# An unused tile that moves the high side of SBUF by 1376 bytes, in a kernel of attention and two MLPs

## The chip, the cores and the metric

The kernel runs on one core of a Trainium2 chip. The core has five engines with queues of their own: TensorE (PE in the rows, with its weight loads as PEld), VectorE (DVE), ScalarE (ACT), GpSimd (POOL) and SyncE (SP), which issues nearly all DMAs here. The engines work on tiles in SBUF, whose 128 partitions each have their own run of bytes, so a tile has one byte address that is the same in all its partitions. TensorE reads a moving and a stationary operand from SBUF and accumulates in PSUM. The metric is the device time of one execution in microseconds (us).

## What is computed

Attention with a feature map (batch 4, 8 heads, 576 rows of 64), then two MLPs on the 2304 rows of 512 that come out of it. In short:

```
phi(x): proj = x @ w_phi; proj -= max|proj| of the row; concat(exp(proj), exp(-proj))
attn:   kv = phi(k)^T v, z = sum of phi(k);  x = (phi(q) kv) / (phi(q) z + 1e-6)
mlp 1:  h = (x @ w1) * (x @ w2);  y = (h @ w3) @ w_out        (512 -> 1024 -> 1024 -> 512)
mlp 2:  r = max(y @ w_in, 0);     out = (r * r) @ w_out2      (512 -> 2048 -> 512)
```

The weights of the MLPs come as 64-bit floats and are taken apart on the chip.

## The kernel before

All of it is one function, `attention_then_mlps`, and the order of instructions on every engine is written out by hand. To keep fp32 accuracy with the faster fp32r matmul, each operand is a tile `[128, 2, 512]` of a high part and a low part, 2048 bytes each. A product is three passes: high by high, low by high, high by low (`passes`). With four blocks of 128 along the contraction, or four blocks of output, that makes **runs of 12 matmuls**, each with a weight load of its own: 128 columns of stationary operand (512 bytes of a partition), then 512 moving columns (256 for the block of the tails).

The work has three stages.

- **Attention**, until about 200 us, with decoding of the first weights beside it.
- **MLP 1**: 40 steps, of which 32 have 512 moving columns and 8 have 256. A step has a run `pa` (L179, in `wide`), a run `pb` (L179) and, one step behind, a run `yp` (L883, in `fold_in`). In the first eight steps there is also `pf` (L840, two runs of 12 in a row), which folds w3 into w_out, and before `yp` the transposes `pw` (L173) for it.
- **MLP 2**: 80 steps, of which 64 have 512 columns and 16 are of the tails. A step has a run `ph` (L179) and, one step behind, `op` (L901, in `last_product`; in the 16 steps of the tails it is only 6 matmuls).

Between the runs, ScalarE and VectorE make the next moving or stationary operand from PSUM: in MLP 2 `t` (L1035), `r` (L1037, L1043 for the high part, L1045 for the low part).

**Where tiles lie.** Pools are opened on one of two sides: the low side is filled from the bottom of SBUF upward, the high side (`side="right"`) from the top downward, and each keeps its buffers from then on. On the low side are the identity matrix, the raw weights and decoding temporaries (`stage`), 20 buffers of 4096 bytes (`units`, made by `unit`) and the 5 operand buffers of `place` (`mid`). On the high side lies first `att` (all that attention needs beyond these) and, when that is closed, `late`: 12 buffers of 4096 bytes, the `t`, `g32` and `g` buffers, and two sets of decoding temporaries.

```python
att = actx.enter_context(tc.tile_pool(name="att", bufs=2, side="right"))
late = ctx.enter_context(tc.tile_pool(name="late", bufs=2, side="right", reuse_waits="tile"))
```

The sides of the operands of each run, by the addresses in the built program (moving, then stationary):

| run | moving operand | stationary operand |
|---|---|---|
| `pa`, `pb` L179 | block of x, low side | w1 or w2, low side |
| `ph` L179 | block of y, low side | w_in, low side |
| `pf` L840 | w_out, low side | w3 turned, low side |
| `yp` L883 | `g`, high side | `w3o` (folded weights), high side |
| `op` L901 | w_out2: 12 of 16 high side, 4 of 16 low side | `r`, high side |

A high part on the low side starts at 2688 modulo 4096, on the high side at 4064 (buffers of 2048 bytes, and all low parts, at 640 and 2016). Both sides have one offset for all their operand tiles of the MLPs.

Of the kernel before, what the change touches and what calls it, by code (L numbers as in the profile page):

```python
# [9 lines left out]
F32 = mybir.dt.float32  # L10
# [7 lines left out]
P = 128  # L18
C = 4
TAIL = 64  # L20
LEFT = 20
RIGHT = 12

# [18 lines left out]
def attention_then_mlps(ctx: ExitStack, tc: tile.TileContext, q, k, v, w_phi, w1, w2, w3, wo, wi2, wo2, out):  # L44
# [15 lines left out]
    units = ctx.enter_context(tc.tile_pool(name="units", bufs=1))  # L60
    mid = ctx.enter_context(tc.tile_pool(name="mid", bufs=1))
    dram = ctx.enter_context(tc.tile_pool(name="dram", bufs=1, space=bass.MemoryType.DRAM))

    def unit(dtype, shape, name):
        return units.tile([P] + shape, dtype, tag="u", bufs=LEFT, name=name)
# [134 lines left out]
    with ExitStack() as actx:  # L200
# [488 lines left out]
        with tc.manual_schedule(engines=mine):  # L689
            for entry in START:  # L690
                name, t = entry.split("/")
# [15 lines left out]

    def lunit(dtype, shape, name, tag="w", bufs=RIGHT):
        return late.tile([P] + shape, dtype, tag=tag, bufs=bufs, name=name)
# [4 lines left out]

    free = {"u": LEFT - 18, "w": RIGHT}
    home, given = {}, []
# [376 lines left out]
```

## Time and profile before

| | |
|---|---|
| device time, median of three runs | 951.58 us (950.89, 951.58, 952.81) |
| the profiled execution: span from first to last instruction | 952.7 us |
| TensorE busy | 931.8 us, 98% |
| VectorE, ScalarE, GpSimd busy | 545.8, 382.4, 249.5 us |
| granted TensorE clock, mean | 0.998 |

Of the profiled execution the page gives the span alone; it lies inside the range of the three runs and 1.1 us above their median. In the rows, a busy TensorE is not yet TensorE at its peak: matmuls overlap, and the length of a row reaches to the modelled end of its last matmul. What a run really takes is the distance from its start to the start of the next run.

### The profile page before, as it was taken

Reading aid. Unit: us, or ns where it says so; the run is one execution under the profiler, and the core shown is the slowest. Engines: PE = TensorE matmul, PEld = TensorE weight load, DVE = VectorE, ACT = ScalarE, POOL = GpSimd, SP = SyncE. Lnnn points to the kernel's source line nnn. Section 1 sums busy time; section 2 is a strip of 40 time slices with the busy share of each in tenths; the row PEclk is TensorE's granted clock in tenths of the full one; section 3 lists DMA queues with packets and bytes.
Section 4 is the critical chain, followed back from the end, with each engine's and each line's share of the span. In section 5 each row is a group of like instructions: output and inputs, shape, how many; then the busy total and the mean of one; then the engine's idle time right before and its main releaser. Section 6 shows DMA issues by size and latency. Waiting matters only on the chain.

```text
span 952.7 us, 14857 instructions
## 1 busy us (share of the span) xinstructions
PE 931.8 (98%) x5915; PEld 764.0 (80%) x5915; DVE 545.8 (57%) x892; ACT 382.4 (40%) x689; POOL 249.5 (26%) x304
## 2 busy tenths in 40 slices
PE   8899998999999999999999999999999999999997
PEld 7677776778888988888988888888888888888896
DVE  5898889778656456666856678852224223322332
ACT  4777777643322333432333344342223223222322
POOL 1565566454121123333423245520000000000000
PEclk9999999999999999999999999999999999999999
DMA  6565566144241334254452333211002000100000
GB/s 166 125 159 151 136 158 199 55 153 157 87 133 55 124 110 155 67 199 155 164 187 91 132 126 96 89 41 48 1 1 89 1 0 1 67 1 1 29 17 22
DMA packets 81109, 89.22 MB, mean 94 GB/s; under 512 B 44624, under 2 KB 65680, under 8 KB 81040
## 3 DMA queue, kind: packets, MB, share of 16 engines
q1 hardware_dynamic: 79712, 87.72, 29.7%
q8 instruction: 46, 0.75, 0.3%
q10 hardware_dynamic: 1328, 0.56, 0.3%
q14 instruction: 23, 0.19, 0.1%
HBM read 69.76 MB, written 18.35 MB: 92 GB/s over the span
## 4 chain that ended last, share of the span: by engine, by line
PE 89%; DVE 4%; ACT 3%; DMA 2%; issue 1%; SPq 0%; ACTq 0%
PE op L901 21%; PE ph L179 21%; PE yp L883 11%; PE pb L179 10%; PE pa L179 10%; PE pf L840 5%; PE po L455 2%; PE pk L246 2%; PE pq L376 2%; PE pkv L428 2%; DMA mrow<-mh 2%; ACT qp L417 2%; PE pd L477 1%; DVE kmax L344 1%; DVE m L383 1%; ACT kp L361 1%
## 5 line engine op out<-in xcount | busy, mean ns | idle before, releaser
L901 PE MATMUL op<-w_w,r 128*128 128x512 f32 x864 | 213.8, 395 | 0.1
L901 PEld LDWEIGHTS op<-w_w,r 128*128 128x128 f32 x864 | 161.3, 188 | 36.8 <-ACT r L1043 0.5
L179 PE MATMUL ph<-y,w_w 128*128 128x512 f32 (+1 forms) x768 | 165.5, 365 | 0.0
L1037 DVE SCALAR_TENSOR_TENSOR r<-ph,t 128x512 f32<-128x512 f32 (+1 forms) x80 | 51.0, 638 | 194.0 <-ACT t L1035 194.0
L179 PEld LDWEIGHTS ph<-y,w_w 128*128 128x128 f32 x768 | 133.3, 188 | 25.8
L1035 ACT ACTIVATE t<-ph 128x512 f32<-128x512 f32 (+1 forms) x80 | 44.5, 556 | 222.2 <-PE ph L179 222.2
L883 PE MATMUL yp<-g,w3o 128*128 128x512 f32 (+1 forms) x480 | 107.6, 373 | 0.0
L883 PEld LDWEIGHTS yp<-g,w3o 128*128 128x128 f32 x480 | 83.8, 188 | 16.0
L125 POOL TENSOR_TENSOR dt_w<-dt_w,dy_w 128x512 f32<-128x512 f32 x48 | 62.9, 1310 | 126.8 <-DVE dy_w L120 126.7
L179 PE MATMUL pa<-c,w_w12a 128*128 128x512 f32 (+1 forms) x432 | 94.4, 368 | 0.0
L179 PE MATMUL pb<-c,w_w12b 128*128 128x512 f32 (+1 forms) x432 | 93.6, 366 | 0.0
L179 PEld LDWEIGHTS pa<-c,w_w12a 128*128 128x128 f32 x432 | 75.1, 188 | 14.2
L179 PEld LDWEIGHTS pb<-c,w_w12b 128*128 128x128 f32 x432 | 75.2, 189 | 13.0
L1045 DVE TENSOR_TENSOR r<-r,r 128x512 fp32r<-128x512 f32 (+1 forms) x80 | 51.0, 638 | 41.3 <-ACT r L1043 35.6
L962 DVE TENSOR_TENSOR g<-pb,a 128x512 f32<-128x512 f32 (+1 forms) x39 | 24.8, 636 | 85.9 <-PE pb L179 81.3
L135 POOL TENSOR_TENSOR w_w<-dt_w,w_w 128x512 fp32r<-128x512 f32 x32 | 48.9, 1528 | 86.8 <-ACT w_w L133 86.8
L1043 ACT ACTIVATE r<-r 128x512 fp32r<-128x512 f32 (+1 forms) x80 | 47.2, 590 | 55.5 <-DVE r L1037 55.5
L502 POOL TENSOR_SCALAR rc<-dc 32x9 f32<-32x9 f32 x128 | 45.4, 355 | 58.8 <-DVE dc L492 51.8
L964 ACT ACTIVATE g<-g 128x512 fp32r<-128x512 f32 (+1 forms) x39 | 23.0, 589 | 91.6 <-DVE g L962 91.6
L954 ACT COPY a<-pa 128x512 f32<-128x512 f32 (+1 forms) x39 | 21.2, 543 | 83.1 <-PE pa L179 83.1
L361 ACT ACTIVATE kp<-kp 128x512 f32<-128x512 f32 (+1 forms) x80 | 46.9, 588 | 17.2 <-DVE kp L354 14.8
L117 DVE TENSOR_SCALAR dy_w<-dt_w 128x512 int32<-128x512 int32 x48 | 51.1, 1064 | 0.7
(135 smaller groups left out, 1285.3 us busy)
## 6 DMA issues: line engine op xcount, KB each, us to landing
x<-x_hbm SPq DMA_DIRECT2D x16, 512.0 KB
raw_w<-in_moe_w_dram SPq DMA_DIRECT2D x16, 512.0 KB
raw_w<-in_moe_w_in_dram SPq DMA_DIRECT2D x16, 512.0 KB
raw_w<-in_moe_w_out_dram SPq DMA_DIRECT2D x16, 512.0 KB
qm<-in_q_dram SPq DMA_DIRECT2D x32, 128.0 KB
km<-in_k_dram SPq DMA_DIRECT2D x16, 256.0 KB
vs<-in_v_dram SPq DMA_DIRECT2D x32, 128.0 KB
raw_wo<-in_moe_w_out_dram SPq DMA_DIRECT2D x8, 512.0 KB
```

Of the source, the lines that this page charges most:

```text
L117: nc.vector.tensor_scalar(out=e, in0=t, scalar1=-(1 << 23), scalar2=None, op0=ALU.bitwise_and)
L125: nc.gpsimd.tensor_tensor(out=w, in0=t.bitcast(F32), in1=e.bitcast(F32), op=ALU.add)
L135: nc.gpsimd.tensor_tensor(out=dst[:, 1], in0=w[0], in1=dst[:, 0].bitcast(F32), op=ALU.subtract)
L179: nc.tensor.matmul(ps[:, 0:n], a, c, start=kk + i == 0, stop=kk == KD - 1 and i == 2)
L361: nc.scalar.activation(z["kp", j][:, :, s, :], z["kp", j][:, :, 1, :], AF.Exp, scale=1.0 - 2.0 * s)
L502: nc.gpsimd.tensor_scalar(out=z["rc2"][i * 32:(i + 1) * 32, s, :], in0=z["dc"][at * 32:(at + 1) * 32, :], scalar1=1e-6, scalar2=None, op0= ...
L840: nc.tensor.matmul(pf, a, c, start=g + j + n == 0, stop=g == 1 and j == 3 and n == 2)
L883: nc.tensor.matmul(blk.yp[i][:, 0:blk.n], a, d, start=c % HG + s == 0, stop=c % HG == HG - 1 and s == 2)
L901: nc.tensor.matmul(ops[i], a, d, start=j + s == 0, stop=j == NR - 1 and s == 2)
L1037: nc.vector.scalar_tensor_tensor(out=r32[:, 0:n], in0=ph[:, 0:n], scalar=0.0, in1=t[:, 0:n], op0=ALU.max, op1=ALU.mult)
L1043: nc.scalar.activation(r[:, 0, 0:n], r32[:, 0:n], AF.Copy)
L1045: nc.vector.tensor_tensor(out=r[:, 1, 0:n], in0=r32[:, 0:n], in1=r[:, 0, 0:n].bitcast(F32), op=ALU.subtract)
```

## The change

A pool `skew` is opened on the high side ahead of all others there, with one tile of 344 floats (1376 bytes of each partition) that nothing writes or reads. As that side is filled downward, every other tile of it lies 1376 bytes lower. The low side, PSUM and the buffers in DRAM stay where they were.

```diff
+SKEW = 344
...
     units = ctx.enter_context(tc.tile_pool(name="units", bufs=1))
     mid = ctx.enter_context(tc.tile_pool(name="mid", bufs=1))
     dram = ctx.enter_context(tc.tile_pool(name="dram", bufs=1, space=bass.MemoryType.DRAM))
+
+    skew = ctx.enter_context(tc.tile_pool(name="skew", bufs=1, side="right"))
+    skew.tile([P, SKEW], F32, name="skew")
```

No instruction is added, removed or moved: on all five engines the order is the same, waits included, with source lines 4 later (L179 is then L183, L883 L887, L901 L905, L840 L844) and other numbers in the names. What differs is the addresses, as the built programs have them:

| tiles | before | after |
|---|---|---|
| low side, operand tiles (high part, low part), modulo 4096 | 2688, 640 | 2688, 640 |
| high side in the MLPs: weights, `g`, `r`, `w3o` (high part, low part), modulo 4096 | 4064, 2016 | 2688, 640 |
| high side in the MLPs: `t`, `a`, `g32`, modulo 4096 | 4064 or 2016 | 2688 or 640 |
| distance of high side to low side, modulo 2048 | 1376 | 0 |
| the same, modulo 64 | 32 | 0 |

In attention the tiles of the high side have many sizes, so they have no single offset before or after; each lies 1376 bytes lower.

## Rows read from the trace of the kernel before

**Rows 1.** The page: busy time, the span in 40 slices, the chain that ended last.

```profile
PE 931.8 (98%) x5915; PEld 764.0 (80%) x5915; DVE 545.8 (57%) x892; ACT 382.4 (40%) x689; POOL 249.5 (26%) x304
...
PEclk9999999999999999999999999999999999999999
...
PE 89%; DVE 4%; ACT 3%; DMA 2%; issue 1%; SPq 0%; ACTq 0%
```

**Rows 2.** Timeline of PE, MLP 1, all operands low: start, length, line, matmuls.

```profile
265.00 2.88 PE L840 MATMUL pf<-w_wo,w3T 128*128 128x512 f32 x12
267.71 2.88 PE L179 MATMUL pa<-c,w_w12a 128*128 128x512 f32 x12
270.44 2.88 PE L179 MATMUL pb<-c,w_w12b 128*128 128x512 f32 x12
273.16 0.38 PE L173 MATMUL pw<-ident,dt_w 128*128 128x128 f32 x2
```

**Rows 3.** Timeline of PE, two steps of MLP 1 without `pf`.

```profile
356.22 2.88 PE L179 MATMUL pb<-c,w_w12b 128*128 128x512 f32 x12
358.94 2.94 PE L883 MATMUL yp<-g,w3o 128*128 128x512 f32 x12
361.72 2.92 PE L179 MATMUL pa<-c,w_w12a 128*128 128x512 f32 x12
364.48 2.89 PE L179 MATMUL pb<-c,w_w12b 128*128 128x512 f32 x12
367.20 1.09 PE L883 MATMUL yp<-g,w3o 128*128 128x512 f32 x4
```

**Rows 4.** Timeline of PE, MLP 2: w_out2 high at 751.98, low at 757.52 and 763.06.

```profile
749.21 2.93 PE L179 MATMUL ph<-y,w_w 128*128 128x512 f32 x12
751.98 2.94 PE L901 MATMUL op<-w_w,r 128*128 128x512 f32 x12
754.75 2.93 PE L179 MATMUL ph<-y,w_w 128*128 128x512 f32 x12
757.52 2.97 PE L901 MATMUL op<-w_w,r 128*128 128x512 f32 x12
760.32 2.90 PE L179 MATMUL ph<-y,w_w 128*128 128x512 f32 x12
763.06 2.97 PE L901 MATMUL op<-w_w,r 128*128 128x512 f32 x12
765.86 0.40 PE L179 MATMUL ph<-y,w_w 128*128 128x512 f32 x1
```

**Rows 5.** Timeline of PE: the first and the last `ph` around MLP 2's 64 steps.

```profile
544.23 1.55 PE L179 MATMUL ph<-c,w_w 128*128 128x512 f32 x6
...
898.79 1.59 PE L179 MATMUL ph<-y,w_w 128*128 128x256 f32 x12
```

**Rows 6.** Timeline of PE, a step of MLP 1 with `pf` (`pa`, `pb`: rows 2).

```profile
262.23 5.64 PE L840 MATMUL pf<-w_wo,w3T 128*128 128x512 f32 x24
...
273.95 3.02 PE L883 MATMUL yp<-g,w3o 128*128 128x512 f32 x12
276.81 5.42 PE L840 MATMUL pf<-w_wo,w3T 128*128 128x512 f32 x23
```

**Rows 7.** Timeline of PE, 256 columns: a step of MLP 1, then the tails of MLP 2.

```profile
321.41 1.60 PE L179 MATMUL pa<-c,w_w12a 128*128 128x256 f32 x12
322.85 1.60 PE L179 MATMUL pb<-c,w_w12b 128*128 128x256 f32 x12
324.29 1.60 PE L883 MATMUL yp<-g,w3o 128*128 128x256 f32 x12
325.73 1.60 PE L179 MATMUL pa<-c,w_w12a 128*128 128x256 f32 x12
...
915.73 1.56 PE L901 MATMUL op<-w_w,r 128*128 128x512 f32 x6
917.12 1.59 PE L179 MATMUL ph<-y,w_w 128*128 128x256 f32 x12
918.55 1.56 PE L901 MATMUL op<-w_w,r 128*128 128x512 f32 x6
```

**Rows 8.** Timeline of DVE, then of ACT, in one step of MLP 2.

```profile
748.72 0.69 DVE L1045 TENSOR_TENSOR r<-r,r 128x512 fp32r<-128x512 f32 x1 [0.70 <-ACT r L1043]
752.87 0.69 DVE L1037 SCALAR_TENSOR_TENSOR r<-ph,t 128x512 f32<-128x512 f32 x1 [3.46 <-ACT t L1035]
...
752.24 0.60 ACT L1035 ACTIVATE t<-ph 128x512 f32<-128x512 f32 x1 [3.55 <-PE ph L179]
```

**Rows 9.** Busy time of PE until 189 us: matmuls, granted clock, DMA share, GB/s.

```profile
0.00:189.00 189.00, 173.77 (x2276) 0.99 0.55 144
```

**Rows 10.** Waits of PE, the two longest: us in total, times, longest.

```profile
PE pq L410 <- DMA mrow<-mh: 7.5, 6, 2.7
PE pq L376 <- ACT qp L417: 3.9, 5, 0.9
```

**Rows 11.** Groups by form, 256 moving columns: attention, then MLP 2 (busy, mean ns).

```profile
L246 PE MATMUL pk<-wbd,kT 128*128 128x256 f32 x192 | 27.0, 290 | 0.0
...
L179 PE MATMUL ph<-y,w_w 128*128 128x256 f32 x192 | 25.4, 282 | 0.0
```

## What was predicted before the run

> **What bounds the kernel now.** I read the page first. TensorE is busy 98% of the span at full granted clock, and the chain that ended last is 89% TensorE [rows 1]. After attention nothing else stands on that chain for long, so from about 200 us on the time is the number of matmuls times what one takes. The question is then what one takes, and whether it hangs on where its operands lie. For that I went to the timeline of TensorE and read it from start to start of the runs, since the length of a row contains the pipeline's end.
>
> There are two paces for the same shape (128x128 weights, 512 columns). **Settled:** from 265.00 to 273.16 stand 36 matmuls in a row (half of `pf`, then `pa`, `pb`), all operands on the low side. They take 8.16 us, 226.7 ns each, though `pf`, `pa` and `pb` have three different weights, two different moving blocks and three PSUM banks [rows 2]. **Disturbed:** a plain step of MLP 1 is also 36 matmuls, `yp` and then `pa` and `pb`, from 358.94 to 367.20: 8.26 us. In it `yp` (high side) takes 2.78, `pa` (low, right behind it) 2.76, and `pb` (low, behind a low run) 2.72 [rows 3]. A run that follows one from the other side is slow; a run that follows one from its own side is not.
>
> MLP 2 alternates low `ph` and high `op` without a second run to settle in. A step takes 5.54 us: 2.77 and 2.77 where both operands of `op` are high (749.21 to 754.75), and 2.80 and 2.74 where its moving operand is low and its stationary one high (757.52 to 763.06) [rows 4]. 24 settled matmuls would be 8.16 x 24/36 = 5.44. Nothing differs between these two kinds of step but the address of w_out2. That moves 0.03 us from one run to the other, which I take as the best sign that addresses of the two operands act on each other.
>
> The Trainium skill speaks against this. In "SBUF — State Buffer", section "Who interferes with whom", TensorE has two independent read ports, one for the moving operand and one for the weights, and never waits for anyone. By that the place of w_out2 could not show, and here it does, by 2.80 against 2.77 [rows 4].
>
> **The change part by part.** It adds no instruction and no wait, and keeps the order of all engines. It moves all tiles of the high side by 1376 bytes, so that operands of both sides have the same offset modulo 2048 (and 64). Every run of the MLPs then stands, modulo 4096, just as the low runs stand to each other in rows 2. I do not know which modulus counts; low runs settle whichever low buffers they use and whichever 512-byte slice of weights comes next, so the modulus that counts divides 512, and by any such modulus the two sides are 352, 96 or 32 bytes apart before and 0 after.
>
> My theory: a pair of operands with different offsets disturbs the overlap of weight load and stream, and after a change of side it takes most of a run to settle again. With one offset there is no change of side. The sum, in differences against the profiled execution's span of 952.7:
>
> - Plain steps of MLP 1 with 512 columns: 8.26 - 8.16 = 0.10 us [rows 2, 3]. There are 32 steps with 512 columns; 8 have `pf`, so 24 x 0.10 = 2.4.
> - Steps with `pf`: the first 24 matmuls of `pf` take 267.71 - 262.23 = 5.48, settled 5.44; `yp` takes 2.86 behind the transposes, settled 2.72 [rows 2, 6]. 0.04 is due to the change of side; of the 0.14 of `yp` I give half to the change of side (0.06 is what a plain `yp` has over 2.72 [rows 3]) and the rest to the transposes ahead of it. 0.10 a step, seven of them (the first lies among attention's last products): 0.7. I count 0.4, since the share of the transposes is a guess.
> - MLP 2 with 512 columns: from 544.23 to 898.79 are 64 steps in 354.56 us [rows 5], 5.54 each, so 64 x (5.54 - 5.44) = 6.4.
> - 256 columns: a step of MLP 1 takes 325.73 - 321.41 = 4.32, 1.44 for each run, the low behind low `pb` too: nothing to gain. A step of the tails in MLP 2 takes 918.55 - 915.73 = 2.82 against 1.44 + 6 x 0.2267 = 2.80 [rows 2, 7]: 16 x 0.02 = 0.3.
> - Attention: there the operands have many offsets before and after. One product has a like in the MLPs: `pk`, moving high, stationary low, 256 columns, has a mean of 290 ns against 282 for `ph` with 256, waits included [rows 11]. 192 x 8 ns = 1.5 us is the most that I give it, on either side of zero, because the settled pace of 256 columns was no better than the disturbed one [rows 7]. TensorE idles 15 us until 189 us [rows 9], partly for DMAs (7.5) and ScalarE (3.9) [rows 10], and a little saved there is lost in those waits. I take 0.
> - VectorE, ScalarE, GpSimd, DMAs: the low part of `r` ends at 749.41 and `op` starts to use it at 751.98 [rows 4, 8]: 2.57 us of cover, so a step that is 0.1 us shorter starves nobody. ScalarE and VectorE wait 3.5 us a step for TensorE [rows 8]. Cost 0; if an elementwise operation took longer at the new addresses, it would have to grow by those 2.57 us in a chain of four operations before it shows.
>
> Sum: 2.4 + 0.4 + 6.4 + 0.3 = 9.5 us. Taken from the median of the runs, 951.6 (the span of the profile is 1.1 above it), that is **942.1**.
>
> **The rivals.** *The switch itself costs, not the address.* Each change of side is also a change from `pre` banks of PSUM to `acc` banks and to operands that were just made. If that causes the 0.10, it stays, and the time is 951.6 within the spread of the runs. For it: the step is 5.54 with w_out2 high or low [rows 4], as if the surplus had a fixed size. Against it: `pf`, `pa`, `pb` change banks and operands and stay at the settled pace, and four banks change inside every `yp` and `op`. This is also where the rule of independent ports from the Trainium skill ("SBUF — State Buffer", "Who interferes with whom") ends up. The Trainium skill, in the same page's section "Specifications (TRN2)", counts in 16-byte lines, and 1376 is 86 of those, so by it no operand changes its place in a line.
>
> *Half of it.* If the high run pays for its own place and the low run for the switch (0.06 and 0.04 of the 0.10 by [rows 3]), only one of the two goes: 951.6 - 4.8 = 946.8.
>
> *Slower.* Equal offsets might be the bad case across the two sides: moving and stationary would then collide in every high run and at each switch. Its price is the pace of the worst run seen, 2.80 for 12 [rows 4]: a step of MLP 2 would take 5.60 and one of MLP 1 8.40, so 64 x 0.06 + 31 x 0.14 = 8.2 and the time 959.8. It turns slower from the point where the mean run takes more than 2.77. Against it: low tiles have exactly this relation to each other, over 20 and more buffers, and settle [rows 2].
>
> That the change doesn't do what it says is no rival: the addresses of the built program moved as described.
>
> **How the numbers follow.** Forecast 0.72 (940.0 to 944.5: each 0.10 is good to 0.01, so 1 us, and attention 1.5), half 0.10 (945 to 949), no change 0.12 (950.5 to 952.8), slower 0.06. A measurement of this kernel tells apart about 0.2%, 1.9 us. Faster by more than that has 0.72 + 0.10 = 0.82, within it 0.12, slower 0.06. The range reaches from 940.0 over the forecast and the half to 948.5, which leaves out the other two, 0.18 together; the forecast's own is 940.0 to 944.5.
>
> **What would show it.** In the profile after, `yp`, `pa`, `ph` and `op` with 512 columns should all take 2.72 from start to start, steps 8.16 and 5.44, and the 64 steps of MLP 2 about 348 us instead of 354.6. `op` with a low w_out2 should look like any other. Attention should end where it ended, within 1.5 us. If steps stay at 8.26 and 5.54, the switch is the cause and not the offset; if `ph` behind `op` stays at 2.76 while `op` falls to 2.72, it is the half. If runs are at 2.80 throughout, equal offsets collide.

## The result, and the profile after

The changed kernel takes 943.39 us (median of 6 runs, 939.63 to 946.28) against 952.19 for the kernel before beside it (6 runs, 950.78 to 953.87). The ratio is 0.9908, with a 95% interval from 0.9889 to 0.9928: 0.9% faster, 8.8 us by the medians. The forecast was 942.1 in a range from 940.0 to 948.5. The profiled execution after has a span of 941.0 and took 942.8.

TensorE's busy time fell by 10.5 us; the busy time of no other engine moved by more than 2 us (compare [rows 1]).

```profile
PE 921.3 (98%) x5915; PEld 762.2 (81%) x5915; DVE 545.7 (58%) x892; ACT 382.6 (41%) x689; POOL 249.6 (27%) x304
```

The timeline of TensorE in MLP 1, after (start, length, line, matmuls; what a run takes is the distance to the next start), answers to [rows 3]:

```profile
338.79 2.88 PE L887 MATMUL yp<-g,w3o 128*128 128x512 f32 x12
341.50 2.88 PE L183 MATMUL pa<-c,w_w12a 128*128 128x512 f32 x12
344.23 2.88 PE L183 MATMUL pb<-c,w_w12b 128*128 128x512 f32 x12
346.94 2.88 PE L887 MATMUL yp<-g,w3o 128*128 128x512 f32 x12
```

`yp`, `pa` and `pb` now have one pace, 2.72 each, and the step is 346.94 - 338.79 = 8.15 or 8.16 instead of 8.26. MLP 2, after, against [rows 4]:

```profile
742.54 2.88 PE L905 MATMUL op<-w_w,r 128*128 128x512 f32 x12
745.26 2.88 PE L183 MATMUL ph<-y,w_w 128*128 128x512 f32 x12
747.99 2.88 PE L905 MATMUL op<-w_w,r 128*128 128x512 f32 x12
750.71 2.88 PE L183 MATMUL ph<-y,w_w 128*128 128x512 f32 x12
753.42 2.88 PE L905 MATMUL op<-w_w,r 128*128 128x512 f32 x12
```

The two steps from 742.54 to 753.42 take 10.88 us, 5.44 each. By the order of steps, w_out2 is high in the `op` at 742.54 and low in those at 747.99 and 753.42; they take the same 2.72. The first `ph` and the start of the tails, against [rows 5]:

```profile
538.54 2.66 PE L183 MATMUL ph<-c,w_w 128*128 128x512 f32 x11
...
886.70 1.60 PE L183 MATMUL ph<-y,w_w 128*128 128x256 f32 x12
```

From 538.54 to 886.70 are 348.16 us for 64 steps, 5.44 each, with w_out2 high or low. That is the settled pace of [rows 2], to 0.01 us, for the whole of MLP 2.

Between the two profiled executions lie 11.7 us, not 8.8, mainly because that of before had a late DMA in attention. The timeline of TensorE before, the clock of that stretch, then the same place after:

```profile
166.86 0.89 PE L410 MATMUL pq<-mrow,minus 128*128 128x512 f32 x3 [2.75 <-DMA mrow<-mh]
167.67 3.48 PE L428 MATMUL pkv<-vs,kp 128*64 128x65 f32 x64
```

```profile
166.00:172.00 6.00, 5.14 (x79) 0.72 0.36 126
```

```profile
165.18 0.76 PE L414 MATMUL pq<-mrow,minus 128*128 128x512 f32 x3 [0.98 <-DMA mrow<-mh]
165.87 2.09 PE L432 MATMUL pkv<-vs,kp 128*64 128x65 f32 x64
```

TensorE's wait was 2.75 instead of 0.98 us. In the 6 us from 166 on the granted clock was 0.72 in the mean, between its two levels of 1.2 and 2.4 GHz (0.5 and 1.0), and `pkv` took 3.48 instead of 2.09: 1.77 + 1.39 = 3.2 us. The old distance alone does not make this DMA late: in a run that has it too (e7 below) no wait for it is longer than 1.2 us. From the start of the first `pf` (203.75 before, 200.57 after) to the start of the last matmul the two executions differ by 9.0 us, close to the 8.8 of the medians; what follows the last matmul was 0.5 us longer after.

### The profile page after: what moved, and what is told of

The parts are those of the page before. It is cut to its first block, busy times and chain, and to the rows that moved or that the text cites. A ratio compares the mean times of both kernels' runs of the same rounds, so it can differ in the third digit from the quotient of the medians.

```text
span 941.0 us, 14857 instructions
## 1 busy us (share of the span) xinstructions
PE 921.3 (98%) x5915; PEld 762.2 (81%) x5915; DVE 545.7 (58%) x892; ACT 382.6 (41%) x689; POOL 249.6 (27%) x304
## 4 chain that ended last, share of the span: by engine, by line
PE 89%; DVE 4%; ACT 3%; DMA 2%; issue 1%; SPq 0%; ACTq 0%
PE ph L183 21%; PE op L905 21%; PE yp L887 11%; PE pb L183 11%; PE pa L183 10%; PE pf L844 5%; PE po L459 2%; PE pk L250 2%; PE pq L380 2%; ACT qp L421 2%; PE pkv L432 2%; DMA mrow<-mh 1%; PE pd L481 1%; DVE kmax L348 1%; DVE m L387 1%; ACT kp L365 1%
## 5 line engine op out<-in xcount | busy, mean ns | idle before, releaser
L905 PE MATMUL op<-w_w,r 128*128 128x512 f32 x864 | 209.6, 390 | 0.1
L905 PEld LDWEIGHTS op<-w_w,r 128*128 128x128 f32 x864 | 161.1, 188 | 33.4 <-ACT r L1047 0.5
L183 PE MATMUL ph<-y,w_w 128*128 128x512 f32 (+1 forms) x768 | 163.9, 362 | 0.0
L183 PEld LDWEIGHTS ph<-y,w_w 128*128 128x128 f32 x768 | 133.3, 189 | 23.8
L887 PE MATMUL yp<-g,w3o 128*128 128x512 f32 (+1 forms) x480 | 106.1, 370 | 0.0
L887 PEld LDWEIGHTS yp<-g,w3o 128*128 128x128 f32 x480 | 83.7, 189 | 14.8
L183 PE MATMUL pa<-c,w_w12a 128*128 128x512 f32 (+1 forms) x432 | 93.6, 366 | 0.0
L183 PE MATMUL pb<-c,w_w12b 128*128 128x512 f32 (+1 forms) x432 | 93.6, 366 | 0.0
L183 PEld LDWEIGHTS pa<-c,w_w12a 128*128 128x128 f32 x432 | 75.1, 189 | 13.2
L183 PEld LDWEIGHTS pb<-c,w_w12b 128*128 128x128 f32 x432 | 75.2, 189 | 13.1
```

The costliest lines, as they stand in the source:

```text
L183: nc.tensor.matmul(ps[:, 0:n], a, c, start=kk + i == 0, stop=kk == KD - 1 and i == 2)
L887: nc.tensor.matmul(blk.yp[i][:, 0:blk.n], a, d, start=c % HG + s == 0, stop=c % HG == HG - 1 and s == 2)
L905: nc.tensor.matmul(ops[i], a, d, start=j + s == 0, stop=j == NR - 1 and s == 2)
```

## Experiments: which distance, and between what

What was open: the change makes the distance between the sides 0 by every modulus at once. The runs vary the size of the unused tile (e1, e2, e4 to e7, e10), put it on the other side (e3), or let weights and `g`, `r` lie apart from each other (e8, e9). A step is read from the profile of one execution (the median of its kind), since whole times scatter by some us with attention while steps of one kind agree to a few nanoseconds within a profile; for a step one run is enough. "High" and "low" say on which side w_out2 lies. "Stretch" is from the start of the first `pf` to the start of the last matmul. The ratios are to runs of the kernel before that were taken beside each experiment (medians 951.6 for e1 to e3, 951.4 for e5).

| unused bytes | distance of the sides, modulo 256 | MLP 2 step, w_out2 high | same, low | MLP 1 step | stretch | time (runs) |
|---|---|---|---|---|---|---|
| none (before) | 96 (1376) | 5.54 | 5.54 | 8.26 | 743.3 | 952.2 (6) |
| 1376 (changed kernel) | 0 | 5.44 | 5.44 | 8.16 | 734.3 | 943.4 (6) |
| 1376, low side (e3) | 0 | 5.44 | 5.44 | 8.16 | 734.3 | 944.8 (6) |
| 96 (e5) | 0 (1280) | 5.44 | 5.44 | 8.16 | 734.3 | 941.7 (7) |
| 1344 (e2) | 32 | 5.51 | 5.53 | 8.23 | 740.3 | 948.3 (10) |
| 1312 (e4) | 64 | 5.49 | 5.55 | 8.21 | 739.8 | 947.4 (1) |
| 32 (e1) | 64 (1344) | 5.49 | 5.55 | 8.21 | 739.8 | 946.5 (9) |
| 1280 (e7) | 96 | 5.54 | 5.54 | 8.26 | 743.3 | 951.8 (1) |
| 1248 (e6) | 128 | 5.46 | 5.55 | 8.18 | 737.8 | 948.0 (1) |
| 1184 (e10) | 192 | 5.49 | 5.47 | 8.21 | 738.5 | 948.6 (1) |

### e1: 32 bytes

```diff
-SKEW = 344
+SKEW = 8
```

> The unused tile is 32 bytes instead of 1376: high and low side are then 1344 bytes apart modulo 2048, a multiple of 64 but not of 128 or 512. Theory A (the distance of the two sides modulo 64 counts): all runs of 12 settle at 2.72 us, a step of MLP 1 takes 8.16, one of MLP 2 5.44, and the time is that of the changed kernel, 943 (941 to 946). Theory B (the distance must vanish modulo 512 or 2048): disturbed steps, 8.2 or more and 5.5 or more, time 950 or more. Theory C (the high side must itself begin on a multiple of 64, whatever the low side does): as A.

Measured: 946.54 (945.81 to 948.16, 9 runs), ratio to the kernel before 0.9947 (0.9930 to 0.9963). The timeline of TensorE in MLP 2:

```profile
742.51 2.89 PE L183 MATMUL ph<-y,w_w 128*128 128x512 f32 x12
745.24 2.92 PE L905 MATMUL op<-w_w,r 128*128 128x512 f32 x12
748.00 2.89 PE L183 MATMUL ph<-y,w_w 128*128 128x512 f32 x12
```

2.73 and 2.76, 5.49 a step: half of the gain. Where w_out2 is low the step is 5.55, so that the whole stretch gains 3.5 of 9.0 us. A and C, both of which had 5.44, fall. B is left, with its sizes missed: it had 5.5 or more a step and 950 or more in time.

### e2: 1344 bytes

```diff
-SKEW = 344
+SKEW = 336
```

> The unused tile is 1344 bytes: the two sides are 32 bytes apart modulo 2048, closer than in any other version but not a multiple of 64. A and C: as the kernel before, 8.26 and 5.54, time 952 (950 to 954). B: also disturbed, since 32 is not 0. A theory D (a coarse distance counts, say a bank of some hundred bytes or more, and 32 bytes are next to nothing): settled, 8.16 and 5.44, 943.

Measured: 948.29 (946.86 to 953.30, 10 runs), ratio 0.9974 (0.9954 to 0.9994).

```profile
743.63 2.91 PE L183 MATMUL ph<-y,w_w 128*128 128x512 f32 x12
746.38 2.92 PE L905 MATMUL op<-w_w,r 128*128 128x512 f32 x12
749.13 2.23 PE L183 MATMUL ph<-y,w_w 128*128 128x512 f32 x9
```

5.50 in this step (5.51 in the median): 32 bytes are enough to lose more than half of the gain (D falls), though not all of it (A and C had 5.54). B had only "disturbed".

### e3: the tile on the low side

```diff
-    skew = ctx.enter_context(tc.tile_pool(name="skew", bufs=1, side="right"))
-    skew.tile([P, SKEW], F32, name="skew")
+    skew = ctx.enter_context(tc.tile_pool(name="skew", bufs=1))
+    skew.tile([P, SKEW], F32, name="skew")
     const = ctx.enter_context(tc.tile_pool(name="const", bufs=1))
```

> The 1376 bytes lie at the bottom of the low side instead of the top of the high side: the two sides have the same offset modulo 2048, but every operand of the MLPs now begins 32 bytes past a multiple of 64. A and B (only the distance counts): settled, 8.16 and 5.44, 943. C (a start at 32 modulo 64 is itself slow): no run settles at 2.72, pa behind pf and pb behind pa included; steps of 8.26 and 5.54 or longer, time 952 or more.

Measured: 944.78 (941.70 to 946.44, 6 runs), ratio 0.9918 (0.9893 to 0.9943), the stretch the same as with the changed kernel to 0.01 us.

```profile
742.60 2.88 PE L905 MATMUL op<-w_w,r 128*128 128x512 f32 x12
745.32 2.88 PE L183 MATMUL ph<-y,w_w 128*128 128x512 f32 x12
748.04 2.88 PE L905 MATMUL op<-w_w,r 128*128 128x512 f32 x12
```

All operands of the MLPs begin at 32 modulo 64 here, and every run takes 2.72. Between this start and that of the changed kernel (224 and 128 modulo 256) it does not matter where a tile begins, only how far the two sides are apart. C falls for good.

### e4: 1312 bytes

```diff
-SKEW = 344
+SKEW = 328
```

> The unused tile is 1312 bytes: the two sides are 64 bytes apart modulo 2048. A and C: settled, 8.16 and 5.44, 943. B: disturbed, since 64 is not 0 modulo 512, 950 or more. With the tile of 32 bytes this tells whether any multiple of 64 will do.

Measured: 947.41 (one run). Every kind of step as in e1 to the nanosecond (`op` 2.762 and 2.798, `ph` 2.732 and 2.748). The distances 64 and 1344 are 1280 = 5 x 256 apart. So the pattern repeats after 1280 bytes. By itself that would also fit 320 or 640; but low runs settle on slices of weights that are 512 bytes apart, as the prediction read from [rows 2], and what divides both 1280 and 512 divides 256. So the modulus is at most 256: B's 512 and 2048 were too coarse, A's 64 too fine. B's time, 950 or more, was missed here too.

### e5, e6, e7: 96, 1248 and 1280 bytes

The edit of e5; in e6 the number is 312, in e7 320:

```diff
-SKEW = 344
+SKEW = 24
```

> The unused tile is 96 bytes: the two sides are 1280 bytes apart, a multiple of 128 and of 256 but not of 512. The steps of MLP 2 so far: 5.54 us at a distance of 1376, 5.50 at 32, 5.49 at 1344 and at 64 (equal to the nanosecond, and 1280 bytes from each other), 5.44 at 0. Theory P128 (only the distance modulo 128 counts): settled, 8.16 and 5.44, time that of the changed kernel, 943.4 (942 to 945). P256: the same. P512 (512 or more): disturbed, 5.49 or more, 947 or more; the equality of 1344 and 64 speaks against it.

Measured: 941.66 (940.83 to 945.87, 7 runs), ratio 0.9901 (0.9880 to 0.9923).

```profile
742.51 2.88 PE L183 MATMUL ph<-y,w_w 128*128 128x512 f32 x12
745.23 2.88 PE L905 MATMUL op<-w_w,r 128*128 128x512 f32 x12
747.95 2.88 PE L183 MATMUL ph<-y,w_w 128*128 128x512 f32 x12
```

Settled throughout with a distance of 1280: P512 falls. The intervals of this kernel and of the changed one overlap nearly entirely, and their stretches are equal, so 96 unused bytes buy what 1376 do.

> The unused tile is 1248 bytes: the two sides are 128 bytes apart. P128: settled, 8.16 and 5.44. P256 and P512: disturbed, 5.45 to 5.54 and 8.2 to 8.3 a step.

Measured: 947.98 (one run).

```profile
741.63 2.89 PE L905 MATMUL op<-w_w,r 128*128 128x512 f32 x12
744.36 2.89 PE L183 MATMUL ph<-y,w_w 128*128 128x512 f32 x12
747.09 2.89 PE L905 MATMUL op<-w_w,r 128*128 128x512 f32 x12
```

2.73 and 2.73: close to settled, but not (5.46), and 5.55 where w_out2 is low. P128 falls and **256** stays; its step of MLP 1, expected at 8.2 to 8.3, took 8.18.

> The unused tile is 1280 bytes: the two sides are 96 bytes apart, which is what 1376 is modulo 128 and 256. P128 and P256: the steps of the kernel before to the nanosecond, 5.54 and 8.26, although every address of the high side is another. P512: some other step.

Measured: 951.82 (one run); `op` 2.777 and 2.808, `ph` 2.763 and 2.732, a step of MLP 1 8.260, all as before. Every address of the high side is 1280 bytes from where it was, and nothing changed.

### e8: the weights in line, `g` and `r` not

```diff
+PAD = 344
...
+                if s == 1:
+                    late.tile([P, PAD], F32, tag="pad", bufs=1, name="pad")
                 a_sb = lunit(F32, [512], f"a_{b}_{c}", "t", 2)
```

This is against the kernel before, so there is no `skew`.

> No tile at the top; an unused tile of 1376 bytes stands inside the pool of the MLPs' high side instead, between the 12 weight buffers and the buffers t, g32, g. The weights of the high side (w_out2, w3o) get the low side's offset, g and r keep the old one. Theory S (the stationary operand's offset counts, when it changes from run to run): op has its stationary operand r 1376 off, so MLP 2 stays at 5.54 in all 64 steps, split 2.81 and 2.73 as where w_out2 was low; yp has its stationary operand w3o in line, so a step of MLP 1 is 8.16. Theory M (the moving operand's): the other way round, 5.44 and 8.26. Theory R (the two operands of one matmul must stand in line): both disturbed, about 5.54 and 8.26.

Measured: 950.52 (one run). MLP 2, and below it a step of MLP 1:

```profile
703.71 2.97 PE L903 MATMUL op<-w_w,r 128*128 128x512 f32 x12
706.52 2.89 PE L181 MATMUL ph<-y,w_w 128*128 128x512 f32 x12
709.25 2.97 PE L903 MATMUL op<-w_w,r 128*128 128x512 f32 x12
```

```profile
362.62 2.98 PE L885 MATMUL yp<-g,w3o 128*128 128x512 f32 x12
365.43 2.92 PE L181 MATMUL pa<-c,w_w12a 128*128 128x512 f32 x12
368.19 2.88 PE L181 MATMUL pb<-c,w_w12b 128*128 128x512 f32 x12
370.91 1.34 PE L885 MATMUL yp<-g,w3o 128*128 128x512 f32 x5
```

`op` takes 2.81 in all 64 steps, as it did before only with a low w_out2; M falls. `yp`, whose stationary operand is in line and whose moving one is not, takes 2.81 as well, more than before (2.78), and the step is 8.29; S falls. R holds: where the two operands of its matmuls are out of line, a run is slow from its first matmul to its last. Lining up the weights alone gained nothing: the stretch is 744.4 us, 1.1 more than before.

### e9: `g` and `r` in line, the weights not

```diff
+SKEW = 24
+PAD = 296
```

with the `skew` of the changed kernel and the `pad` of e8.

> The other half of the pad experiment: 96 bytes unused at the top and 1184 between weights and t, g32, g. Now g and r are in line with the low side (1280 apart, 0 modulo 256) and the high side's weights stand 96 off, as 1376 is modulo 256. Theory R (the two operands of one matmul must stand in line): op takes 2.81 and its ph 2.73 where w_out2 is high (12 of 16), and both take 2.72 where w_out2 is low (4 of 16), the reverse of the kernel before; yp has w3o off and takes 2.81, a step of MLP 1 8.29. Theory S (only a change of the stationary operand's offset counts; r and w_in are in line now): 5.44 in all 64 steps of MLP 2, and 8.26 in MLP 1, where w3o is off. Theory M fell with the run before: with w_out2 in line throughout, MLP 2 stayed at 5.54.

Measured: 950.49 (one run). MLP 2 with a low w_out2 at 720.44 and a high one at 725.88:

```profile
717.68 2.92 PE L184 MATMUL ph<-y,w_w 128*128 128x512 f32 x12
720.44 2.88 PE L906 MATMUL op<-w_w,r 128*128 128x512 f32 x12
723.16 2.88 PE L184 MATMUL ph<-y,w_w 128*128 128x512 f32 x12
725.88 2.98 PE L906 MATMUL op<-w_w,r 128*128 128x512 f32 x12
728.69 1.55 PE L184 MATMUL ph<-y,w_w 128*128 128x512 f32 x6
```

```profile
363.34 2.97 PE L888 MATMUL yp<-g,w3o 128*128 128x512 f32 x12
366.15 2.89 PE L184 MATMUL pa<-c,w_w12a 128*128 128x512 f32 x12
...
371.60 0.62 PE L888 MATMUL yp<-g,w3o 128*128 128x512 f32 x2
```

As R had it, the low w_out2 is now the good one: `op` 2.72 and the `ph` behind it 2.72, against 2.81 for the high one. `yp` is 2.81 with w3o out of line. Two sizes were off: `ph` behind a slow `op` takes 2.76, not 2.73, and the step of MLP 1 is 8.26, not 8.29, since `pa` is back at its pace sooner (2.73) than in e8 (2.76). A step of MLP 2 with a high w_out2 comes to 5.57, more than in the kernel before. So it is not one fixed price for a switch; which of the two operands is off decides where it falls. `op` and `yp` agree on that over the kernel before, e8 and e9: with the moving operand off the run takes 2.815 and the low run behind it 2.76, with the stationary one off 2.808 and 2.73. The stretch, 743.3, is that of the kernel before.

### e10: 1184 bytes

```diff
-SKEW = 344
+SKEW = 296
```

> The unused tile is 1184 bytes: the two sides are 192 bytes apart, 64 short of 256. Steps of MLP 2 so far by distance modulo 256: 5.44 at 0, 5.50 at 32, 5.49 at 64, 5.54 at 96, 5.46 at 128. If the sign of the distance does not matter (high and low change places at each switch, so each sign comes once a step): the same as at 64, 5.49. If it does: between 5.44 and 5.54, another number.

Measured: 948.57 (one run).

```profile
741.68 2.90 PE L905 MATMUL op<-w_w,r 128*128 128x512 f32 x12
744.41 2.92 PE L183 MATMUL ph<-y,w_w 128*128 128x512 f32 x12
747.17 2.89 PE L905 MATMUL op<-w_w,r 128*128 128x512 f32 x12
```

5.49 as at 64, but the other way round: 2.73 for `op` and 2.76 for `ph` (at 64, 2.76 and 2.73). Over the two switches of a step the sign cancels. In the steps with a low w_out2, where one sign alone counts, it does not: 5.47 here, 5.55 at 64.

### One matmul at a time

The starts of single matmuls in the traces show how a switch costs what it does. Nanoseconds from one matmul's start to the next, the 12 of a run (the runs start at 702.12, 704.89, 757.52 and 760.32 before, 697.76 in e10, 742.54 after):

```
op, before, both operands high      236 233 237 223 231 236 229 231 231 227 227 236
ph behind it                        229 234 236 224 231 235 230 231 231 227 226 229
op, before, w_out2 low, r high      230 233 237 237 231 234 236 232 232 238 237 231
ph behind it                        232 231 227 227 226 227 227 226 227 227 227 228
op, distance 192 (e10)              229 233 231 226 227 227 226 227 227 226 227 225
op, after                           226 227 227 226 227 227 226 227 227 226 227 227
```

A weight load runs while the matmul ahead of it streams. In the trace before, the loads of the `op` whose first matmul starts at 768.60 begin 0.23 us earlier, when the last matmul of `ph` starts:

```profile
768.37 2.76 PEld L901 LDWEIGHTS op<-w_w,r 128*128 128x128 f32 x12
```

In the first two lines both operands of a run are on one side and in line. What is out of line is only the first load of a run, which meets the moving operand of the other side; and 236, the last distance of the first line, is the one that ends with the start of `ph`. So R in its words, the two operands of one matmul, is too narrow: it would leave these two runs undisturbed. The pair that fits is a moving operand and the weights that are loaded while it streams, the next matmul's. After one such load it takes up to nine matmuls to come back to 227, along nearly the same numbers each time (236, 224, 231, 236, 228, 233, 231, 226, 227); a distance that disturbs less enters that row further on (e10). In a run whose own operands are out of line every load is one, and it never comes back (third line). The settled pace is 2720 / 12 = 226.7 ns, 544 cycles of 2.4 GHz for 512 columns (the granted clock is 1.00 there).

## Why the prediction was right, step by step

**The theory held, and its modulus is now known.** At the distances tried, the settled pace came where the operand that streams and the weights that are loaded meanwhile are a multiple of 256 bytes apart, and nowhere else. The prediction had bounded the modulus by 512 from above, and 256 divides that. (Its "352, 96 or 32" leaves out moduli of 32 and less, by which the sides were in line already; had one of them counted, nothing would have changed.) That it is the overlap of load and stream which suffers is not shown by itself: a weight load's row is 188 ns long before and after, and only the distance between the starts of matmuls grows.

**Its size, by stages.** From the traces of before and after:

- MLP 2, 64 steps: 354.56 to 348.16, 6.40. Predicted 6.4.
- Steps with `pf`: from the first `pf` to the first `pa` with 256 columns 107.70 (203.75 to 311.45) and 107.27 (200.57 to 307.85), 0.43. Predicted 0.4. Below is one of them after, against [rows 6]: `pf` fell from 5.48 to 5.44. `yp` behind the transposes took 2.86 or 2.88 in turn and now takes 2.84 (here) or 2.82: 0.04 less on average and not 0.07, so most of its surplus over 2.72 stays although nothing is out of line; it was put down to the transposes ahead, which no run takes away. Two of the eight `pf`, the first (5.57, then 5.61) and the fourth (5.51, then 5.52), gained nothing. 0.4 came out by the cut that was made for this doubt, which is in part luck.

```profile
258.86 5.60 PE L844 MATMUL pf<-w_wo,w3T 128*128 128x512 f32 x24
264.30 2.88 PE L183 MATMUL pa<-c,w_w12a 128*128 128x512 f32 x12
...
270.54 3.01 PE L887 MATMUL yp<-g,w3o 128*128 128x512 f32 x12
273.38 1.98 PE L844 MATMUL pf<-w_wo,w3T 128*128 128x512 f32 x8
```

- The other steps of MLP 1: from there to the first `ph` 232.78 and 230.69, 2.09. Predicted 2.4. Twenty plain steps gave their 0.10; the four that border on a block of 256 columns gave next to nothing, since a 512 run behind a 256 run still takes 2.75 (329.17 - 326.42):

```profile
322.10 1.60 PE L183 MATMUL pa<-c,w_w12a 128*128 128x256 f32 x12
...
326.42 2.91 PE L183 MATMUL pa<-c,w_w12a 128*128 128x512 f32 x12
329.17 2.20 PE L183 MATMUL pb<-c,w_w12b 128*128 128x512 f32 x9
```

- The tails of MLP 2: 45.18 (898.79 to 943.97) and 45.10 (886.70 to 931.80), 0.08. Predicted 0.3. Step by step nothing changed, 2.82 as in [rows 7]. This term was mis-sized: it priced 6 matmuls at the settled pace, 1.36 us, and with nothing out of line they still take 1.38 (to the next `ph` at 904.98). There every run is a change of columns, as in the run of 2.75 above; no run separates that from other causes.

```profile
903.60 1.55 PE L905 MATMUL op<-w_w,r 128*128 128x512 f32 x6
...
906.42 1.55 PE L905 MATMUL op<-w_w,r 128*128 128x512 f32 x6
```

In sum 9.0 instead of 9.5, off by the last two terms. Attention was taken at 0, and nothing shows otherwise: over all kernels here the start of the first `pf` lies between 198.9 and 205.8 with no order by distance, and `pk` moved from 290 to 288 ns. The cover of `r` was never needed. The step that compared the profile with the median was off: the span of 952.7 was set against the runs' times, but a run's time is mostly about 1.8 us more than its span (941.0 and 942.8 after; up to 3.4 in a few runs), so the profiled execution of before was a long one by some 3 us, which is the size of that late DMA. The sum was made as a difference and did not suffer from it.

**The rivals.** *The switch itself* fell with the result: banks, pools and fresh operands still change at every run, at 2.72. What had spoken for it, the step of 5.54 with w_out2 high and low alike, is a coincidence of the distance 96: at 64 the two kinds take 5.49 and 5.55, at 128 5.46 and 5.55. *Half of it* and *slower* did not come. That other engines' reads and writes of the moved tiles cause it, which the prediction did not weigh, falls with e9: there `op` takes 2.72 or 2.81 within one execution, and only the address of w_out2 differs, which by then TensorE alone reads. The rule of two independent read ports (the Trainium skill, "SBUF — State Buffer", "Who interferes with whom") is not what these traces show for a pair of operands: with the same ports, instructions and order, `op` takes 2.72 or 2.81 by the distance alone (e9). Whether the ports, or the memory behind them, cause it, no run here tells. The 16-byte lines of the same page ("Specifications (TRN2)") don't explain it either: every distance tried is a multiple of 16.

**Still open**: why a single mismatched load disturbs up to nine matmuls, and whether a distance that is not a multiple of 32 would behave otherwise, since tiles here begin at multiples of 32. Whether it matters for bf16 or plain fp32 products was not tried.

## What to carry to other kernels

Where TensorE is busy all the time, read its runs from start to start and compare runs of equal shape; if one pace is lower than another, look up the addresses of both operands. Here, for fp32r matmuls that load weights each time, moving and stationary tiles whose addresses differ by a multiple of 256 bytes gave 226.7 ns a matmul and others up to 235 in the mean of a run (2.815 us for 12), and a handful of unused bytes at the start of one side of SBUF (96 do as well as 1376) set it right for the whole kernel. When two candidate causes come out at the same total, change the size of one before believing either: equal totals at one distance were chance.

## What was not expected of the hardware

- The effect repeats with 256 bytes, not with 64, 128 or 512: step times are equal to the nanosecond at distances of 64 and 1344, and of 96 and 1376, and low runs settle on slices 512 bytes apart.
- A distance of 128 nearly settles a step (5.46), 32 and 64 cost half to two thirds of the worst (5.51 and 5.49), 96 the most (5.54), all with both operands of `op` high; it is no matter of far and near. With w_out2 low, 64 and 128 cost the most (5.55).
- A change of the number of columns disturbs as well, with no change of side: the 512 run behind a 256 run takes 2.75 instead of 2.72 in the changed kernel too, and why stays open.
